# Skip term as a scalar in the frequency product, and a program order for the first six chunks

## The chip, the cores and the metric

The kernel runs on one core of a Trainium2 chip. The core has a matrix engine (PE, with its weight loads PEld), a vector engine (DVE), an activation engine (ACT), a general engine (POOL) and a queue engine (SP). Engines run at the same time, each goes through its own instructions in order, and they meet at semaphores. Transfers are issued from queues (here SP's and POOL's) and done by 16 DMA engines. The metric is the device time of one execution in microseconds (us); the time before is 758.68 us, the median of 3 runs (758.16 to 759.4).

## The reference, cut to what matters

One block of a conditioned network over 2048 positions and 512 channels: a layer norm with a modulation, a state-space convolution with a skip term, a residual, a second layer norm, and a two-layer MLP.

```python
mod = (silu(c) @ w_mod).reshape(1, 6, 1, -1)        # six rows: sa, ca, ga, sb, cb, gb
h = layernorm(x) * (1 + ca) + sa
# the convolution, per channel d:
P = exp(logdA[:, :, None] * l)                       # 128 complex states, 2048 positions
K = einsum("dn,dnl,dn->dl", Cc, P, dB).real          # its kernel
y = irfft(rfft(pad(h)) * rfft(pad(K)))[:L] + h * Dskip
x = x + ga * y
h = layernorm(x) * (1 + cb) + sb
x = x + gb * (mish(h @ w1 + b1) @ w2)                # w1 512x1792, w2 1792x512
```

The skip `h * Dskip` can be had in three ways that are the same in exact arithmetic: added to the output, added to the kernel's first tap (K[0] + Dskip), or added to every frequency of the kernel's transform (a first tap of height Dskip has the constant transform Dskip).

## The kernel before, in words

The kernel is written in Python for a scheduler: each line issues an instruction with tiles, and the scheduler works out the order of each engine from the data it needs and from a priority number (low first), then adds the waits. A tile pool gives each tag a fixed number of buffers; who wants a buffer waits for the last reader of the tile that held it.

**Stages.** (1) Parameters of the state space are prepared on DVE and ACT for each of four blocks b of 128 channels (`params`, stages 0 to 3, `load_s`, `coarse`). (2) The convolution is done in 32 chunks, 8 for each block. (3) The MLP, from about 436 us on, is matmuls with fp32 operands split in two parts.

**A slot.** The loop over k from -1 to 40 is the slot loop. In slot k each step of `ORDER` runs for the chunk k minus its offset:

- `ang` (chunk k+2): PE matmuls that make 2 x 512 angles in PSUM (one buffer of two banks, "pa"), L343 and L347.
- `sin` (k+2): three ACT passes, Abs (L354) and two sines (L138), into the tile `ec` (three buffers).
- `mag` (k+1): two DVE products m2 and m1 (L364, L367).
- `comb` (k): four DVE multiplies of `ec` by the magnitudes (L374 to L378).
- `kgen` (k-1): 64 small PE matmuls that give 16 channels' kernels (L389).
- `ks` (k-1): ACT copies them out of PSUM (L394), and DVE adds the skip to the first tap (L395).
- `ka` (k-1): the first half of the kernel's transform on PE (L406), and `tm` copies it (ACT, L413).
- `gl` (offset 6), `ubu` (7), `ug` (7): load the first half of the input's transform from DRAM (`ud`), do its second half on PE (L522, with a shift term at L529), and scale it on ACT into the tile `ug` (two buffers).
- `ubk` and `prod` (8): the second half of the kernel's transform (PE, tile `pkb`), and the complex product of both on DVE: two multiplies at L556 and a subtraction and an addition.
- `t1`, `invb`, `zl`, `xp`, `inva`: transposes (L563) and the inverse transform, through DRAM, with the residual.

**The input's first half.** Ahead of slot 7 the input x (2048 rows as 16 tiles `XR`) is loaded by 20 transfers (`x_rows`, L189), its mean and variance are taken (`stats`: three quarters by DVE's statistics instructions L671 and L672, the fourth quarter by ACT's accumulating passes L677 and L681), `norm_scales` makes the reciprocal roots by twelve small DVE instructions, `norm` scales each of the 16 tiles (L495), and `ua`, eight groups, does 16 matmuls each (L502), four ACT copies (L506) and eight stores to `ud` from SP (L508). The eight copies of two groups have a buffer each; the third group waits for the first one's stores.

**The modulation.** Each of six rows of 512 needs four loads of w_mod (`mod_load`, L430), four products on PE of two matmuls each (`mod_mm`, L437), a copy (`mod_cp`), four small products (`mod_sum`, L446) and a DVE copy (L447). Rows 3 and 0 are needed for the input's scale, row 5 for the shift (`shift_ratio`, `shift_rows`).

**What sets the order.** `MS` gives each modulation row its slot, `SL` the slots of the parameter stages within a block of eight, `BN`, `NS`, `UO` those of statistics, norms and `ua`. Work dealt out so (`extra`) runs in the groups "misc" and "par". The tables `PRI0` (slots below 7) and `PRI` (from 7 on) shift the priority number of a step within its slot. Every engine's order is then the scheduler's.

Of the kernel before, what the change touches and what calls it, by code (L numbers as in the profile page):

```python
# [10 lines left out]
F32 = mybir.dt.float32  # L11
# [7 lines left out]
P = 128  # L19
# [94 lines left out]
def s4_block(ctx, tc, io, out):  # L114
    nc = tc.nc
    V, A, T = nc.vector, nc.scalar, nc.tensor
# [31 lines left out]
    def view(src, offset, ap):  # L148
        return bass.AP(tensor=src.tensor, offset=src.offset + offset, ap=ap)
# [82 lines left out]
    def params(b, stage):  # L232
# [9 lines left out]
        def split(i, j):  # L242
            hi = PKR[b][:, 2 * i:2 * j:2, :]
            (A.copy if b and SPA else V.tensor_copy)(hi, r[:, 10 + i:10 + j, :])
            V.tensor_sub(PKR[b][:, 2 * i + 1:2 * j:2, :], r[:, 10 + i:10 + j, :], hi)
# [146 lines left out]
    def s_ks(k):  # L392
        KS[k] = gen.tile([P, 256], F32, tag="ks", name=f"ks{k}", bufs=1)
        A.copy(KS[k], PK[k][:, :256])  # L394
        V.tensor_add(KS[k][:, 0:256:64], KS[k][:, 0:256:64], dtap[:, k])  # L395
# [27 lines left out]
    WM, PM = {}, {}  # L423
# [15 lines left out]
    def mod_cp(s):  # L439
        WM[s] = cv.tile([P, D], F32, tag="q2", name=f"mr{s}", bufs=1)  # L440
        A.copy(WM[s], PM[s])

    def mod_sum(s):
        p = bank("pmodp")
        for b in range(NB):
            T.matmul(p[:, b:b + 1], WM[s][:, b * P:b * P + P], mean, start=True, stop=True)  # L446
        V.tensor_scalar(modp[:, s, :], p[:, :NB], float(s in (2, 3)), None, op0=OP.add)  # L447
# [84 lines left out]
    def alt(tag, v):  # L532
        pool = MW["wr"] if "wr" in MW and v % 2 else cv
        return pool.tile([P, 512], F32, tag=tag, name=f"{tag}{v}", bufs=1)

    def s_ug(v):
        b = v // 8
        UG[v] = cv.tile([P, 512], F32, tag="ug", name=f"ug{v}", bufs=NUG).rearrange("p (r c s) -> p r c s", r=4, c=2)
        A.mul(UG[v].rearrange("p r c s -> p c r s"), PU[v].rearrange("p (c r s) -> p c r s", c=2, r=4),
              gd[:, b:b + 1])  # L540
# [7 lines left out]
    def s_prod(v):  # L548
        b = v // 8
        ug = UG[v]  # L550
        q1 = alt("q1", v).rearrange("p (r c s) -> p r c s", r=4, c=2)
        q2 = cv.tile([P, 4, 2, 64], F32, tag="q2", name=f"q2{v}", bufs=1)
        YY[v] = q1
        kv = PKB[v].rearrange("p (c r s) -> p c r s", c=2, r=4)
        for q, c in ((q1, 0), (q2, 1)):
            V.tensor_mul(q, kv[:, c, :, None, :].to_broadcast([P, 4, 2, 64]), ug)  # L556
        V.tensor_sub(q1[:, :, 0], q1[:, :, 0], q2[:, :, 1])
        V.tensor_add(q1[:, :, 1], q1[:, :, 1], q2[:, :, 0])
# [86 lines left out]
    s_sin(0)  # L645
    s_mag(0)
# [44 lines left out]
    at(-1, lambda: nc.sync.dma_start(mf.rearrange("p a b -> p (a b)"), io["mf"]))  # L691
    for g in range(4):
        at(BN[g], stats, g)
    at(NS, norm_scales)
    at(2, lambda: nc.sync.dma_start(mi.rearrange("p a b -> p (a b)"), io["mi"]))
# [90 lines left out]
    for nm, o in ORDER:  # L786
        if nm in ("par", "misc"):
            STEPS.append((nm, nm, 0))
        else:
            STEPS.append((nm, locals()["s_" + nm], o))  # L790

    NAME = {params: "p", load_s: "ls", norm: "nr", ua: "ua", mod_load: "ml", mod_mm: "mm", mod_cp: "mc", mod_sum: "ms",
# [3 lines left out]
    def run(name, k, pos, f, *a):  # L796
        tc.cur_priority = 100000 + int(10000 * (k + (PRI0 if k < KP else PRI).get(name, pos)))
        f(*a)

    def run_extra(k, group, pos):  # L800
        for g, a in extra.get((k, group), []):
            run(NAME.get(g, "ld"), k, pos, g, *a)

    for k in range(-1, last_slot + 1):
        if k == NG + 2:
            mlp_open()
        for i, (nm, f, o) in enumerate(STEPS):
            pos = i / len(STEPS)
            if isinstance(f, str):
                if k >= LATE:  # L810
                    run_extra(k, f, pos)
                continue
            if (0 if k >= 0 else 1) <= k - o < (NG - 4 if f in (s_xp, s_zl, s_inva) else NG):
# [121 lines left out]
_INS = ["A_u", "B_w1", "B_b1", "B_w2", "c", "w_mod"]  # L935
# [34 lines left out]
```

## Time and profile before

| what | value |
|---|---|
| median of 3 runs | 758.68 us (758.16 to 759.4) |
| the profiled execution's own time | 760.26 us |
| its span in the trace | 758.5 us, 14126 instructions |
| busy: PE, DVE, ACT, POOL | 662.4, 434.8, 339.2, 51.7 us |
| weight loads (PEld) | 510.4 us |
| moved by DMA | 82.92 MB |

The span is what the trace covers; what lies around it is 1.8 us. Busy times are sums over the whole span, and the stages have different limits, so they say little by themselves. A line of a timeline has the start in us, the duration of the whole group in us, engine, source line, operation, tiles written and read with their shape, and the count of instructions merged; in brackets stands the idle time ahead of it and what ended that idle time. Matmuls overlap, so a group's duration is less than count by mean. A line of a group has busy us and mean ns of one, then idle time ahead of the group in sum. A line of DMA issues has the count, the size of each and the median us from issue to landing. A line of a stage has its bounds, its length, and for PE, PEld, DVE, ACT and POOL the busy us with the count of instructions, then the granted clock of PE, the DMA engines' share and GB/s.

### The profile page before, as it was taken

The page shows a single profiled execution, that of the slowest core. Times are in us where ns is not written, and L with a number is a line of the kernel's source. Part 1 is how long each engine was busy: PE and PEld are TensorE (multiplying, and loading weights), DVE is VectorE, ACT ScalarE, POOL GpSimd, SP SyncE. Part 2 cuts the span into 40 slices and gives each one's busy share as a digit, 9 for nine tenths or more (in the row PEclk, how much of TensorE's full clock was granted, in tenths as well). Part 3 has the DMA queues.
Part 4 walks back from the last instruction along what each step waited for, and adds up shares of the span by engine and source line. Part 5 has one row for each costly group of instructions (what it writes and reads, how often), then busy time and mean ns, then how long its engine had stood idle before and what let it go on. Part 6 is the DMA issues. An engine that isn't in the chain of part 4 may idle for free.

```text
span 758.5 us, 14126 instructions
## 1 busy us (share of the span) xinstructions
PE 662.4 (87%) x5696; PEld 510.4 (67%) x5696; DVE 434.8 (57%) x900; ACT 339.2 (45%) x529; POOL 51.7 (7%) x111
## 2 busy tenths in 40 slices
PE   0661997899999999999883699999999999999995
PEld 0431435567877878887663278887888888878884
DVE  6598626597999988996562596137211521152113
ACT  3760558555786677665441163232223322232220
POOL 1024002050206020000000000000000000000000
PEclk9875879899999999999997799999999999999998
DMA  9925588653326662654965770003200320002002
GB/s 229 237 97 176 136 186 188 181 135 105 76 63 146 160 178 81 166 153 143 262 174 143 211 254 15 1 4 88 75 1 0 89 79 0 1 11 74 1 1 55
DMA packets 98489, 82.92 MB, mean 109 GB/s; under 512 B 11636, under 2 KB 79992, under 8 KB 97784
## 3 DMA queue, kind: packets, MB, share of 16 engines
q1 hardware_dynamic: 91704, 78.15, 37.6%
q0 software_dynamic: 6720, 3.87, 2.7%
q8 instruction: 45, 0.74, 0.4%
q14 instruction: 20, 0.16, 0.1%
HBM read 54.72 MB, written 25.17 MB: 105 GB/s over the span
## 4 chain that ended last, share of the span: by engine, by line
PE 76%; DMA 7%; DVE 6%; ACT 6%; SPq 3%; issue 2%; POOL 0%; DVEq 0%; ACTq 0%; POOLq 0%
PE pm L864 18%; PE po L882 18%; PE pang L343 4%; PE pub L522 4%; PE pkg L389 4%; PE pka L406 4%; PE pang L347 4%; PE pkb L522 4%; PE pib L571 4%; PE pt L563 2%; PE pmodr L437 2%; ACT ec L354 2%; PE pua L502 1%; DMA raw<-in_par 1%; PE pia L609 1%
## 5 line engine op out<-in xcount | busy, mean ns | idle before, releaser
L871 DVE TENSOR_TENSOR mal<-mh,mah 128x512 fp32r<-128x512 f32 x56 | 38.6, 691 | 178.7 <-ACT mah L870 178.2
L864 PE MATMUL pm<-hh,w1h 128*128 128x512 f32 x448 | 138.6, 390 | 2.2 <-ACT hh L775 1.2
L138 ACT ACTIVATE mh<-pm,b 128x512 f32<-128x512 f32 x56 | 38.5, 690 | 202.5 <-PE pm L864 202.5
L864 PEld LDWEIGHTS pm<-hh,w1h 128*128 128x128 f32 x448 | 83.7, 188 | 21.6 <-ACT hh L775 2.1
L882 PE MATMUL po<-w2h,mah 128*128 128x512 f32 x224 | 87.8, 392 | 0.0
L882 PE MATMUL po<-w2h,mal 128*128 128x512 f32 x224 | 87.7, 391 | 0.0
L882 PE MATMUL po<-w2l,mah 128*128 128x512 f32 x224 | 87.5, 391 | 0.0
L864 PE MATMUL pm<-hh,w1l 128*128 128x512 f32 x224 | 87.2, 389 | 0.0
L406 PE MATMUL pka<-bdk,ks 128*64 128x128 f32 x512 | 39.0, 285 | 17.9 <-DVE ks L395 17.9
L556 DVE TENSOR_TENSOR q<-pkb,ug 128x512 f32<-128x512 f32 x64 | 41.2, 685 | 21.8 <-PE pkb L522 21.6
L374 DVE TENSOR_TENSOR ec<-ec,m 128x1024 f32<-128x1024 f32 x32 | 39.1, 1221 | 20.2 <-ACT ec L138 19.9
L882 PEld LDWEIGHTS po<-w2h,mal 128*128 128x128 f32 x224 | 42.1, 188 | 8.8 <-DVE mal L871 0.3
L864 PEld LDWEIGHTS pm<-hh,w1l 128*128 128x128 f32 x224 | 42.0, 188 | 8.6
L882 PEld LDWEIGHTS po<-w2l,mah 128*128 128x128 f32 x224 | 42.1, 188 | 8.4
L882 PEld LDWEIGHTS po<-w2h,mah 128*128 128x128 f32 x224 | 42.1, 188 | 8.3
L406 PEld LDWEIGHTS pka<-bdk,ks 128*64 128x64 f32 x512 | 29.3, 139 | 24.5 <-DVE ks L395 18.4
L354 ACT ACTIVATE ec<-pang 128x1024 f32<-128x1024 f32 x32 | 33.0, 1030 | 26.6 <-PE pang L343 23.5
L347 PE MATMUL pang<-rnd,oneb 128*128 128x512 bf16 x128 | 43.0, 420 | 0.0
L343 PE MATMUL pang<-ac,s 128*128 128x256 f32 x128 | 31.0, 325 | 13.2 <-ACT ec L138 13.0
L364 DVE TENSOR_TENSOR m<-co 128x1024 f32<-128x1024 f32 x32 | 39.1, 1222 | 2.9 <-ACT co L138 2.4
L571 PE MATMUL pib<-yt,mi 128*128 128x128 f32 x256 | 36.6, 288 | 4.5 <-ACT yt L565 4.5
L343 PE MATMUL pang<-nac,s 128*128 128x256 f32 x128 | 40.2, 397 | 0.0
(165 smaller groups left out, 1140.9 us busy)
## 6 DMA issues: line engine op xcount, KB each, us to landing
ud<-us SPq DMA_DIRECT2D x64, 128.0 KB, 2.4
gu<-ud SPq DMA_DIRECT2D x32, 256.0 KB, 3.5
zd<-z SPq DMA_DIRECT2D x32, 256.0 KB, 2.6
zt<-zd SPq DMA_DIRECT2D x32, 256.0 KB, 4.8
wm<-in_w_mod SPq DMA_DIRECT2D x24, 256.0 KB, 3.5
out<-ot SPq DMA_DIRECT2D x64, 64.0 KB, 1.7
xp<-in_A_u SPq DMA_DIRECT2D x60, 64.0 KB, 2.5
x2d<-xp SPq DMA_DIRECT2D x15, 256.0 KB, 3.7
```

The lines of the kernel that those rows point to most:

```text
L343: T.matmul(p[:, e, 256 * q:256 * q + 256], S12[b, 2 * q + c // 4][:, e, :], w[:, 32 * o:32 * o + 256], start=(w is ac and q == 0), stop=(w ...
L347: T.matmul(p[:, e, :], oneb.to_broadcast([P, P]), rnd[:, z:z + 1].to_broadcast([P, 512]), start=False, stop=False, skip_group_check=True)
L354: A.activation(ang[0], pv, AF.Abs)
L364: V.tensor_mul(m2.rearrange("p d (a b) -> p d a b", a=8), co[:, :, 12:20, None].to_broadcast([P, 16, 8, 8]), co[:, :, None, 20:28].to_broa ...
L374: V.tensor_mul(ec[:, :, :, 32:64], ec[:, :, :, 95:63:-1], m2[:, None, :, 0:32].to_broadcast([P, 2, 16, 32]))
L406: T.matmul(pv[64 * cc:64 * cc + 64, :, o:o + 4], KS[k][:, 64 * m:64 * m + 64], bdk[:, 128 * cc:128 * cc + 128], start=True, stop=True)
L522: T.matmul(pv[:, :, r, :], lh(r), mf[:, 4 * s + r, :].rearrange("p (c s) -> p c s", c=2), start=not started, stop=True, skip_group_check=s ...
L556: V.tensor_mul(q, kv[:, c, :, None, :].to_broadcast([P, 4, 2, 64]), ug)
L571: T.matmul(p[:, P * r:P * r + P], mi[:, 4 * s + r, :], YT[v][:, r, :], start=True, stop=True)
L864: T.matmul(p, w1[wi][:, k, fs], hh[:, hi, k, :], start=(n == 0), stop=(n == 3 * KB - 1))
L871: V.tensor_sub(a[1], h, a[0])
L882: T.matmul(PO[tt][q], a[ai][:, P * q:P * q + P], w2[wi][:, f, :], start=(f == 0 and n == 0), stop=(f == FB - 1 and n == 2))
```

## The change

1. **Skip.** `dtap` with its memset and load, and the add at L395, are gone. A tile `skip` holds Dskip as one value per channel and block. `s_prod` uses it as the scalar of one multiply: (kernel + skip) * input.
2. **Layout of the product.** `ug` keeps PSUM's order of real and imaginary parts, and the product's result is written back into the `ug` tile, which `t1` then reads. Before, it was written into `q1`.
3. **Program order.** The wrapper `InOrder` ties every DVE, ACT and PE instruction to the one issued before it on the same engine, from behind `stats(3)` until slot 6 begins (`KO`). The ties carry no wait; they only fix the engine's order. In these slots the steps follow `FIRST`. From slot 6 on `ORDER` and `PRI` hold; `PRI0` is gone.
4. **Work dealt out by slot.** `stats` of all quarters and `norm_scales` stand ahead of the slots. `NR` deals the norms to slots 0, 0, 1, 1, 2, 3, 3, 3 and `UA` the eight ua groups to slots 1, 1, 2, 3, 3, 4, 5, 5. Modulation rows go to slots 1, 2, 3 (rows 3, 5, 0) and 8, 10, 12 (1, 2, 4), each with its loads one slot before and its copy, sum and DVE copy one, two and three slots behind; before, they were 0, 1, 3 and 6, 8, 9. The shift goes from slot 5 to 6, the loads of the transform's tables `mf` and `mi` from slots -1 and 2 to 3 and 5.
5. **Parameters.** In each block stage 2 goes from slot 0 to 1, stage 3 from 2 to 3, the first `load_s` from 5 to 4.
6. **Loads of x.** Every second transfer of the first load of x is issued from POOL's queue instead of SP's.

```diff
+SL = {"p2": 1, "p3": 3, "ls0": 4, "raw": 2, "p0": 5, "ls1": 8, "co0": 6, "vis": 6}
+MS = [[3, 1], [5, 2], [0, 3], [1, 8], [2, 10], [4, 12]]
+MR = 6
+NR = [0, 0, 1, 1, 2, 3, 3, 3]
+UA = [1, 1, 2, 3, 3, 4, 5, 5]
+KO = 6
+FIRST = [
+    ("kgen", 1), ("ks", 1), ("ang", -2), ("comb", 0), ("mag", -1), ("sin", -2), ("ka", 1), ("tm", 1),
+    ("gl", 6), ("misc", 0), ("par", 0),
+]
...
+            def issue(*a, **kw):
+                ins = f(*a, **kw)
+                if self.key in ordered:
+                    if ordered[self.key] is not None:
+                        tc.add_manual_dep(ins.ins, ordered[self.key].name,
+                                          mybir.DependencyInfo(mybir.DependencyClass.NoSync,
+                                                               mybir.DependencyReason.DATA),
+                                          reason="program order")
+                    ordered[self.key] = ins.ins
+                return ins
...
+    V, A, T = InOrder(nc.vector, "V"), InOrder(nc.scalar, "A"), InOrder(nc.tensor, "T")
...
-    dtap = cst.tile([P, 8 * NB, 4], F32, name="dtap")
-    nc.gpsimd.memset(dtap, 0.0)
-    nc.sync.dma_start(dtap[0:P:32], io["dtap"].rearrange("t (k m) -> t k m", m=4))
+    skip = cst.tile([P, NB], F32, name="skip")
+    nc.sync.dma_start(skip, view(io["A_Dskip"], 0, [[1, P], [P, NB]]))
...
+            q = nc.gpsimd if b is None and a % 2 else nc.sync
...
-        V.tensor_add(KS[k][:, 0:256:64], KS[k][:, 0:256:64], dtap[:, k])
...
+        ug = UG[v].rearrange("p (c x) -> p c x", c=2)
+        y = YY[v] = UG[v].rearrange("p (r c s) -> p r c s", r=4, c=2)
+        V.scalar_tensor_tensor(q1, kv[:, 0:1].to_broadcast([P, 2, 256]), skip[:, b:b + 1], ug,
+                               op0=OP.add, op1=OP.mult)
+        V.tensor_mul(q2, kv[:, 1:2].to_broadcast([P, 2, 256]), ug)
+        V.tensor_sub(y[:, :, 0], rs(q1[:, 0]), rs(q2[:, 1]))
+        V.tensor_add(y[:, :, 1], rs(q1[:, 1]), rs(q2[:, 0]))
...
-    s_sin(0)
-    s_mag(0)
...
+    at(3, lambda: nc.sync.dma_start(mf.rearrange("p a b -> p (a b)"), io["mf"]))
+    stats(3)
+    for key in "VAT":
+        ordered[key] = None
+    s_sin(0)
+    s_mag(0)
+    for g in (1, 2, 0):
+        stats(g)
+    norm_scales()
+    at(5, lambda: nc.sync.dma_start(mi.rearrange("p a b -> p (a b)"), io["mi"]))
...
+        if k == KO:
+            ordered.clear()
```

More of the change, by code (lines that the diff above doesn't have):

```diff
@@ L115, in s4_block, with __init__, __getattr__ @@
     nc = tc.nc
-    V, A, T = nc.vector, nc.scalar, nc.tensor
+    ordered = {}
+    class InOrder:
+        def __init__(self, engine, key):
+            self.engine, self.key = engine, key
+        def __getattr__(self, name):
+            f = getattr(self.engine, name)
+            def issue(*a, **kw):
[8 more added lines that the diff above has]
+                return ins
+            return issue
+    V, A, T = InOrder(nc.vector, "V"), InOrder(nc.scalar, "A"), InOrder(nc.tensor, "T")
     psum = ctx.enter_context(tc.tile_pool(name="psum", bufs=6, space=bass.MemoryType.PSUM))
@@ L243, in split @@
             hi = PKR[b][:, 2 * i:2 * j:2, :]
-            (A.copy if b and SPA else V.tensor_copy)(hi, r[:, 10 + i:10 + j, :])
+            V.tensor_copy(hi, r[:, 10 + i:10 + j, :])
             V.tensor_sub(PKR[b][:, 2 * i + 1:2 * j:2, :], r[:, 10 + i:10 + j, :], hi)
@@ L421, in s4_block @@
     nc.gpsimd.memset(one, 1.0)
-    WM, PM = {}, {}
+    WM, PM, MRW = {}, {}, {}
     mean = cst.tile([P, 1], F32, name="mean")
@@ L439, in mod_cp @@
     def mod_cp(s):
-        WM[s] = cv.tile([P, D], F32, tag="q2", name=f"mr{s}", bufs=1)
-        A.copy(WM[s], PM[s])
+        MRW[s] = cv.tile([P, D], F32, tag="q2", name=f"mr{s}", bufs=1)
+        A.copy(MRW[s], PM[s])
     def mod_sum(s):
@@ L445, in mod_sum, with mod_out @@
         for b in range(NB):
-            T.matmul(p[:, b:b + 1], WM[s][:, b * P:b * P + P], mean, start=True, stop=True)
-        V.tensor_scalar(modp[:, s, :], p[:, :NB], float(s in (2, 3)), None, op0=OP.add)
+            T.matmul(p[:, b:b + 1], MRW[s][:, b * P:b * P + P], mean, start=True, stop=True)
+        PM[s] = p
+    def mod_out(s):
+        V.tensor_scalar(modp[:, s, :], PM[s][:, :NB], float(s in (2, 3)), None, op0=OP.add)
     sab = cst.tile([P, D], BF16, name="sab")
@@ L537, in s_ug @@
         b = v // 8
[L538 to L540 removed]
+        UG[v] = cv.tile([P, 512], F32, tag="ug", name=f"ug{v}", bufs=NUG)
+        A.mul(UG[v], PU[v], gd[:, b:b + 1])
     def s_ubk(v):
@@ L549, in s_prod @@
         b = v // 8
[L550 to L558, printed above, removed]
+        ug = UG[v].rearrange("p (c x) -> p c x", c=2)
+        y = YY[v] = UG[v].rearrange("p (r c s) -> p r c s", r=4, c=2)
+        q1 = alt("q1", v).rearrange("p (c x) -> p c x", c=2)
+        q2 = cv.tile([P, 2, 256], F32, tag="q2", name=f"q2{v}", bufs=1)
+        kv = PKB[v].rearrange("p (c x) -> p c x", c=2)
+        V.scalar_tensor_tensor(q1, kv[:, 0:1].to_broadcast([P, 2, 256]), skip[:, b:b + 1], ug,
+                               op0=OP.add, op1=OP.mult)
+        V.tensor_mul(q2, kv[:, 1:2].to_broadcast([P, 2, 256]), ug)
+        rs = lambda t: t.rearrange("p (r s) -> p r s", r=4)
+        V.tensor_sub(y[:, :, 0], rs(q1[:, 0]), rs(q2[:, 1]))
+        V.tensor_add(y[:, :, 1], rs(q1[:, 1]), rs(q2[:, 0]))
     def s_t1(v):
@@ L690, in s4_block @@
     at(-1, const_loads)
[L691 to L695, printed above, removed]
+    at(3, lambda: nc.sync.dma_start(mf.rearrange("p a b -> p (a b)"), io["mf"]))
[8 more added lines that the diff above has]
+    at(5, lambda: nc.sync.dma_start(mi.rearrange("p a b -> p (a b)"), io["mi"]))
     for i, n in MS:
         for q in range(KB):
-            at(max(n - 1 + q // 2, -1), mod_load, KB * i + q)
-            at(n + q // 2, mod_mm, KB * i + q)
+            at(n - 1, mod_load, KB * i + q)
+            at(n, mod_mm, KB * i + q)
         at(n + 1, mod_cp, i)
-        at(n + 1, mod_sum, i)
+        at(n + 2, mod_sum, i)
+        at(n + 3, mod_out, i)
     at(MR, shift_ratio)
@@ L718, in s4_block @@
         for h in range(2):
-            at(NS, norm, 8 * h + g)
-        at(NS + UO + n // 2, ua, g)
+            at(NR[n], norm, 8 * h + g)
+        at(UA[n], ua, g)
     def mlp_open():
@@ L785, in s4_block @@
     STEPS = []
[L786 to L792, printed above, removed]
+    steps = lambda order: [(nm, nm if nm in ("par", "misc") else globals_[f"s_{nm}"], o) for nm, o in order]
+    globals_ = locals()
+    FS, STEPS = steps(FIRST), steps(ORDER)
+    NAME = {params: "p", load_s: "ls", norm: "nr", ua: "ua", mod_load: "ml", mod_mm: "mm", mod_cp: "mc", mod_sum: "ms", mod_out: "ms",
             shift_ratio: "sr", shift_rows: "sr", stats: "st", norm_scales: "no", coarse_mm: "co", visit: "vi",
@@ L806, in s4_block @@
             mlp_open()
-        for i, (nm, f, o) in enumerate(STEPS):
+        if k == KO:
+            ordered.clear()
+        for i, (nm, f, o) in enumerate(FS if k < KO else STEPS):
             pos = i / len(STEPS)
             if isinstance(f, str):
[L810 to L813, printed above, removed]
+                run_extra(k, f, pos)
+            elif (0 if k >= 0 else 1) <= k - o < (NG - 4 if f in (s_xp, s_zl, s_inva) else NG):
                 run(nm, k, pos, f, k - o)
-        for n in ("par", "misc") if k < LATE else ():
-            run_extra(k, n, 0.99)
         if k == last_slot - 3:
@@ L932, in s4_block @@
         fin_q(3, q, xl)
[L935 removed]
+_INS = ["A_u", "A_Dskip", "B_w1", "B_b1", "B_w2", "c", "w_mod"]
 _PAR = ["A_B_re", "A_B_im", "A_C_re", "A_C_im", "A_A_re", "A_A_im"]
```

18 lines of the change are left out of this document (3 added, 15 removed).

## The prediction

> **What bounds the kernel now.** I read the slices of the span first, then busy time by stage, then the engines' timelines through the first stages, and last SP's queue.
>
> ```profile
> span 758.5 us, 14126 instructions
> PE   0661997899999999999883699999999999999995
> ```
> ```profile
> 49.50:126.14 76.64, 53.85 (x617) 28.18 (x614) 49.59 (x111) 35.77 (x59) 16.22 (x32) 0.80 0.64 163
> 182.83:355.60 172.77, 170.02 (x2602) 140.44 (x2605) 158.92 (x265) 123.85 (x186) 20.49 (x40) 1.00 0.49 128
> ```
>
> The first fence has PE's busy tenths in slices of 19 us: nines from the tenth slice on, but for the passage to the MLP (slices 20 to 23). The second gives for a stretch the busy time of PE, its weight loads, DVE, ACT and POOL, then the granted clock. In the steady stage, from 182.83 on, PE is busy 170.0 of 172.8 us at full clock. There the change can give little, for it adds and removes no matmul. The head is another matter: 76.6 us pass from the first kernel chunk (kgen(0), 49.50) to the sixth (kgen(5), 126.14), with PE busy in 53.9 of them at a mean clock of 0.80.
>
> DVE's timeline says why; the second fence is ACT and PE:
>
> ```profile
> 27.73 0.68 DVE L367 TENSOR_TENSOR m<-co 128x512 f32<-128x512 f32 x1
> 34.60 1.23 DVE L374 TENSOR_TENSOR ec<-ec,m 128x1024 f32<-128x1024 f32 x1 [6.19 <-ACT ec L138]
> 38.08 0.69 DVE L376 SCALAR_TENSOR_TENSOR ec<-ec,m 128x512 f32<-128x512 f32 x1
> 53.85 1.28 DVE L671 BATCH_NORM_STATS2 bst<-xr 128x6 f32<-128x512 f32 x2
> 65.16 7.62 DVE L495 TENSOR_SCALAR xr<-xr,mv,rstd 128x512 f32<-128x512 f32 x16
> ```
> ```profile
> 49.50 1.15 PE L389 MATMUL pkg<-ec 128*32 128x64 f32 x64
> 50.70 0.37 ACT L394 COPY ks<-pkg 128x256 f32<-128x256 f32 x1 [3.12 <-PE pkg L389]
> 72.91 0.69 PE L406 MATMUL pka<-bdk,ks 128*64 128x128 f32 x2 [16.75 <-DVE ks L395]
> 126.14 1.17 PE L389 MATMUL pkg<-ec 128*32 128x64 f32 x64
> 142.91 1.17 PE L389 MATMUL pkg<-ec 128*32 128x64 f32 x64
> 144.33 1.16 PE L522 MATMUL pub<-mf,gu 128*128 128x128 f32 x8
> ```
>
> ACT has the first chunk's ks ready at 51.1. The skip term's small add stands on DVE behind the statistics, the scales and all sixteen norms (53.85 to 72.78), and PE waits 16.75 us for it. Only then can the eight ua groups come, in a heap, and SP must store their rows:
>
> ```profile
> 82.90 24.15 SPq L508 DMA_DIRECT2D ud<-us  x32
> 108.42 23.67 SPq L508 DMA_DIRECT2D ud<-us  x32
> 135.72 1.92 PE L437 MATMUL pmodr<-wm,sc 128*32 128x512 f32 x2 [5.30 <-DMA wm<-in_w_mod]
> 140.49 1.52 PE L437 MATMUL pmodr<-wm,sc 128*32 128x512 f32 x4
> ```
>
> 64 stores at 0.75 us hold SP from 82.9 to 132.1. Weights of the modulation queue behind them (PE waits 5.30 for those), and the first ubu, which needs all of ud, does its products at 144.33.
>
> **The change, part by part.**
>
> *Skip term.* The add at L395 goes, and with it DVE's place between ks and ka. The product takes the scalar instead: one of its two multiplies becomes a three-operand instruction with a pointer.
>
> ```profile
> L556 DVE TENSOR_TENSOR q<-pkb,ug 128x512 f32<-128x512 f32 x64 | 41.2, 685 | 21.8 <-PE pkb L522 21.6
> L467 DVE SCALAR_TENSOR_TENSOR sa_a<-sab,hl,pmod 128x512 f32<-128x512 bf16 x1 | 0.7, 747 | 2.7 <-ACT sab L466 2.7
> ```
>
> The nearest row with a pointer and PSUM costs 747 against 685 ns: 62 ns by 32 chunks is 2.0 us more of DVE at worst, none at best. In the steady stage DVE is busy 158.9 of 172.8 us and PE has 2.7 us idle, so neither reaches the end: nothing.
>
> *UG keeps the product.* A UG buffer is now free only when the transposes t1 have read it. In a steady slot:
>
> ```profile
> 182.83 1.17 PE L389 MATMUL pkg<-ec 128*32 128x64 f32 x64
> 185.44 0.69 ACT L539 ACTIVATE ug<-pub,gd 128x512 f32<-128x512 f32 x1 [1.02 <-DVE ks L395]
> 187.08 0.60 PE L563 MATMUL pt<-ident,q 128*128 128x128 f32 x4
> 187.28 1.02 ACT L354 ACTIVATE ec<-pang 128x1024 f32<-128x1024 f32 x1 [1.15 <-PE pang L343]
> 190.62 1.17 PE L389 MATMUL pkg<-ec 128*32 128x64 f32 x64
> ```
>
> ug(v+2), at 185.44, moves behind t1(v), which ends at 187.68. Its reader is the product a slot of 7.8 us (182.83 to 190.62) later; that slack hides it: nothing. Without the cover, with ug still queued ahead of Abs, ACT is 187.68 + 0.69 - 187.28 = 1.1 us late in each slot: rival C.
>
> *The start in program order.* DVE now does mag(0), twelve statistics and the scales, and only then comb(0): 28.4 (27.73 + 0.68) and 11.3 (53.85 to 65.16) make 39.7, against 34.60 before. comb(0) takes 4.2 (34.60 to 38.77), so kgen(0) can come at 43.9. ACT's statistics of the fourth quarter may stand ahead of the first sines as well, and PE does ang(2) before kgen(0): I take 46, between 44 and the 49.5 of before. x has to be there in time for this: two statistics take 1.4 with what is between them, so the last four start at 28.4 + 4 x 1.4 = 34.
>
> *Slots 1 to 5.* Each has one kernel chunk; the ua groups are 2, 1, 2, 1, 2; three modulation rows, the norms and params lie between. DVE's work, cut up, fits into each slot. What is left is a chain over PE and ACT:
>
> ```profile
> 129.33 1.09 PE L406 MATMUL pka<-bdk,ks 128*64 128x128 f32 x14
> 52.04 1.03 ACT L354 ACTIVATE ec<-pang 128x1024 f32<-128x1024 f32 x1
> 115.49 2.27 PE L502 MATMUL pua<-xr,bdu 32*64 32x512 f32 x24
> 117.49 3.52 ACT L506 COPY us<-pua 128x512 f32<-128x512 f32 x7 [1.08 <-PE pua L502]
> ```
>
> kgen and ang on PE 3.2 (126.14 to ka at 129.33), the three sine passes 3.0 (1.03 each, overlapping a little), the copies tm and mod_cp 0.5 each, eight ua copies 4.0 (seven took 3.52), ks 0.4: 11.6. With one ua group it is 9.6. Three and two of them: 54, so kgen(5) stands at 100. Low end: PE's own work alone. Five times kgen, ang, ka (4.3), three modulation rows of eight matmuls (0.38 each at 140.49; 9) and eight ua of 16 matmuls (1.5 each; 12) are 42.5: kgen(5) at 88.5. High end: the pace at which chunks came while ua copies crowded ACT:
>
> ```profile
> 100.17 0.17 DVE L395 TENSOR_TENSOR ks<-ks,dtap 128x4 f32<-128x4 f32 x1 [5.55 <-ACT ks L394]
> 114.00 0.17 DVE L395 TENSOR_TENSOR ks<-ks,dtap 128x4 f32<-128x4 f32 x1 [6.45 <-ACT ks L394]
> ```
>
> 13.8 by five is 69: kgen(5) at 115. I take 100, for that chain follows the order as it is written out.
>
> *To the first ubu.* kgen(6) follows a slot with table loads and eight exponentials; the like slot later takes 10.6 (206.20 to 216.80), and ubu's products start 1.4 behind kgen (142.91 to 144.33): 112. The other condition is the rows of ud. Slot 5's first ua copy is 4.4 ahead of kgen(5), at 96; sixteen stores of 0.75, landing 2.4 and gu 3.5 give 114. I take 115.
>
> ```profile
> 206.20 1.17 PE L389 MATMUL pkg<-ec 128*32 128x64 f32 x64
> 216.80 1.17 PE L389 MATMUL pkg<-ec 128*32 128x64 f32 x64
> ud<-us SPq DMA_DIRECT2D x64, 128.0 KB, 2.4
> gu<-ud SPq DMA_DIRECT2D x32, 256.0 KB, 3.5
> mf<-in_mf SPq DMA_DIRECT2D x1, 2048.0 KB, 11.6
> mi<-in_mi SPq DMA_DIRECT2D x1, 2048.0 KB, 8.1
> ac<-in_ac POOLq DMA_DIRECT2D x1, 512.0 KB, 7.7
> s<-pk POOLq DMA_DIRECT2D x16, 16.0 KB, 2.8
> ```
>
> *Moved rows and loads.* Modulation rows 1, 2 and 4 go to slots 8, 10 and 12. Of row 1, six matmuls stood ahead of 144.33 (135.72 and 140.49) and now come behind it: 3.4 at the clock of those rows, half of it at the full clock; I take 1.5. mf and mi move from the start to slots 3 and 5, among the stores: nothing while the stores keep ahead of the copies, 20 us of transfers if not (rival B). skip's load is 512 single floats in front of the second raw load, where dtap had four long rows: 0 to 2, I take 1. Params move by a slot in each block: DVE has 13.9 us free in 172.8, nothing.
>
> *The sum.* 144.3 - 115 = 29.3, less 1.5 and 1: 26.8 us. The profiled execution took 760.26 (its span 758.5), so 733.5 for such a one; it stands 1.6 above the median of the runs, 758.68, which gives **732**. With kgen(5) at 88.5 the stores allow ubu(0) at 102: 40 us gained, 719. With 115 it is at 127: 15 gained, 744.
>
> **The rivals.**
>
> *B: the stores stay the bound.* The first ua copy stands 7.6 behind kgen(0), at 54. From there 64 stores of 0.75 (48), mf 11.6, mi 8.1 and 5.9 to gu make 128 for the first ubu; with eight weight loads at two stores' time each (12) 140. Middle 134: 10.3 less 2.5 gained, **751**. For it: SP needed 49 us for the stores alone, and its queue is in order: the third raw load, in slot 2, must wait there for params of slot 3. Against: spread over slots of 54 us the stores have gaps to hide in.
>
> *C: the longer life of UG.* 1.1 us in each of 22 slots (172.8 / 7.8) is 24; half of that covered, 12: **744**. Against: ACT has 49 of 172.8 us free, and ACT's order behind the sixth chunk is dealt out anew with this wait known.
>
> *D, the other side: x comes late.* Half of x's twenty loads go to POOL's queue, and DVE in program order cannot pass the statistics. Every microsecond that x lands after 34 is one for all that follows; from 34 + 26.8 = 61 on the kernel is slower. If the ten landed one after the other, at the 7.7 us of a POOL load in this window, from 3 on, they end at 80, 46 late: **778**. Against: POOL's loads overlap, and between 52 and 72 us, with DVE full of statistics and norms, sixteen small ones landed in 2.8 us each (the last row above).
>
> The Trainium skill speaks for D: by "SBUF — State Buffer", section "SBUF: two separate sides", GpSimd cannot write the descriptors of its own DMAs while DVE runs a fast two-port operation, and the remedy named is the queue that these loads leave. The row of 2.8 us does not show such a hold-up.
>
> *E: nothing gained.* If program order adds 5 us to each of the five slots, because ACT, waiting for a us buffer, keeps ks and the sines behind it, kgen(5) is where it was: **759**.
>
> **How the numbers follow.** Forecast 0.60, B 0.20, C 0.09, D 0.06, E 0.05. The forecast's own range is 719 to 744. To hold 8 in 10 I keep 719 below and go over B to 754 above; D, E and tails are left out. A difference under 0.2% (1.5 us) counts as no change. Faster is the forecast, B and C less their tails, 0.87; same is most of E, 0.04; slower is D and the rest of E, 0.09.
>
> **What would show it.** No PE wait near 17 us ahead of the first ka; kgen(5) between 88 and 115 and the first ubu between 102 and 127; no stretch of DVE with all statistics and norms in one piece; the first store ahead of 65; a steady slot of 7.8 us. Wrong: DVE idle on x's loads ahead of the statistics; ACT waiting on ud for over 15 us in sum; PE waiting on gu or weights past 127; steady slots over 8.2.

## The result, and the profile after

The changed kernel takes 737.96 us (median of four runs, 736.02 to 740.05) against 758.42 of the kernel before (757.17 to 759.4): a ratio of 0.973, with a 95% interval of 0.969 to 0.977. The sum said 732, and faster. The sign is right, the time lies in the range, and the gain is 20.5 us where the sum had 26.8. The profiled execution of after took 740.05, its span is 738.2.

The first fence holds the head of the page and PE's busy tenths; the second, busy time by stage (columns as in the prediction).

```profile
span 738.2 us, 14029 instructions
PE   0449877999999999999955899999999999999995
```
```profile
54.66:111.38 56.72, 48.63 (x632) 27.41 (x637) 55.93 (x108) 36.39 (x60) 16.28 (x32) 0.89 0.75 182
161.17:334.00 172.83, 167.91 (x2567) 139.39 (x2586) 157.08 (x242) 121.57 (x185) 21.43 (x42) 1.00 0.51 132
```

The steady stage is what it was. From kgen(0) to kgen(5) pass 56.7 us instead of 76.6, and in them DVE is busy 55.9. But that stretch begins 5.2 us later than before, at 54.66 instead of 49.50. All three engines' instructions now bear the line of the wrapper, L126, so one reads by tile names. DVE's and PE's timelines, and ACT's last cast of the shift rows:

```profile
19.46 0.42 DVE L126 TENSOR_TENSOR raw<-raw 128x256 f32<-128x256 f32 x1 [7.49 <-DMA raw<-in_par]
36.77 1.83 DVE L126 TENSOR_TENSOR m<-co 128x1024 f32<-128x1024 f32 x2 [2.84 <-ACT co L126]
50.92 1.94 DVE L126 TENSOR_TENSOR ec<-ec,m 128x1024 f32<-128x1024 f32 x2
```
```profile
111.38 1.47 PE L126 MATMUL pkg<-ec 128*32 128x64 f32 x64
118.78 1.17 PE L126 MATMUL pkg<-ec 128*32 128x64 f32 x64
122.31 0.80 PE L126 MATMUL pang<-ac,s 128*128 128x256 f32 x2 [2.35 <-ACT ec L126]
128.04 0.50 PE L126 MATMUL pang<-ac,s 128*128 128x256 f32 x2 [2.03 <-ACT ec L126]
131.40 1.69 PE L126 MATMUL pub<-mf,gu 128*128 128x128 f32 x8
134.05 1.17 PE L126 MATMUL pkg<-ec 128*32 128x64 f32 x64
337.33 1.17 PE L126 MATMUL pkg<-ec 128*32 128x64 f32 x64
```
```profile
129.43 0.61 ACT L126 CAST sab<-sa_a 128x512 bf16<-128x512 f32 x1
```

In the first fence the second raw tile is late (19.46; before, the first multiply on it stood at 11.50), and with it all that follows up to the first comb (50.92). In the second, the first ubu comes only at 131.40, 12.6 behind kgen(6). The last chunk, kgen(31), stands at 337.33; before, it stood here:

```profile
355.53 1.17 PE L389 MATMUL pkg<-ec 128*32 128x64 f32 x64
```

So 18.2 us are gained ahead of kgen(31), and the rest of the span differs by 2.1 (402.97 before, 400.87 after). That rest has the last products in it, whose form the change alters; from the last product on, where the code is the same, it is 350.2 and 350.3. Over the fourteen kernels profiled here the rest behind kgen(31) lies between 397.7 and 403.0. Each kernel's runs spread by 2 to 10 us. So below I read the time by its interval, and use the starts in the trace to see which step moved.

SP's queue, the stores of ua's rows and the first loads of gu:

```profile
64.47 12.07 SPq L531 DMA_DIRECT2D ud<-us  x16
79.42 4.62 SPq L531 DMA_DIRECT2D ud<-us  x7
85.99 19.61 SPq L531 DMA_DIRECT2D ud<-us  x25
108.94 11.72 SPq L531 DMA_DIRECT2D ud<-us  x16
123.63 0.94 SPq L537 DMA_DIRECT2D gu<-ud  x2
```

The stores are four bursts with gaps now, and end at 120.7 instead of 132.1.

### The profile page after: what moved, and what is told of

Read it like the earlier page. It is cut to its first block, busy times and chain, and to the rows that moved or that the text cites. A ratio compares the mean times of both kernels' runs of the same rounds, so it can differ in the third digit from the quotient of the medians.

```text
span 738.2 us, 14029 instructions
## 1 busy us (share of the span) xinstructions
PE 651.5 (88%) x5667; PEld 509.2 (69%) x5696; DVE 433.3 (59%) x868; ACT 336.1 (46%) x529; POOL 56.5 (8%) x120
## 4 chain that ended last, share of the span: by engine, by line
PE 73%; DVE 12%; DMA 7%; ACT 3%; issue 2%; SPq 1%; DVEq 0%; ACTq 0%
PE pm L126 21%; PE po L126 20%; PE pang L126 6%; PE pub L126 5%; PE pkg L126 4%; PE pkb L126 4%; PE pib L126 3%; DVE ec L126 3%; PE pka L126 3%; DVE raw L126 3%; DMA raw<-in_par 2%; PE pt L126 2%; PE pia L126 1%; PE pln L126 1%; DMA wm<-in_w_mod 1%
## 5 line engine op out<-in xcount | busy, mean ns | idle before, releaser
L126 DVE TENSOR_TENSOR mal<-mh,mah 128x512 fp32r<-128x512 f32 x56 | 38.6, 691 | 181.2 <-ACT mah L126 180.8
L126 PE MATMUL pm<-hh,w1h 128*128 128x512 f32 x448 | 139.5, 393 | 1.1 <-ACT hh L126 1.1
L126 ACT ACTIVATE mh<-pm,b 128x512 f32<-128x512 f32 x56 | 38.5, 690 | 202.5 <-PE pm L126 201.7
L126 DVE TENSOR_TENSOR ec<-ec,m 128x1024 f32<-128x1024 f32 (+1 forms) x96 | 97.2, 1040 | 13.9 <-ACT ec L126 13.6
L126 PEld LDWEIGHTS pm<-hh,w1h 128*128 128x128 f32 x448 | 84.7, 190 | 19.7 <-ACT hh L126 1.5
L126 ACT ACTIVATE ec<-pang 128x1024 f32<-128x1024 f32 x64 | 65.0, 1033 | 58.6 <-PE pang L126 58.6
L126 PE MATMUL po<-w2h,mah 128*128 128x512 f32 x224 | 87.8, 392 | 0.0
L126 PE MATMUL pm<-hh,w1l 128*128 128x512 f32 x224 | 87.7, 391 | 0.0
L126 PE MATMUL po<-w2h,mal 128*128 128x512 f32 x224 | 87.6, 391 | 0.0
L126 PE MATMUL po<-w2l,mah 128*128 128x512 f32 x224 | 87.5, 391 | 0.0
L126 DVE TENSOR_TENSOR m<-co 128x512 f32<-128x512 f32 (+1 forms) x64 | 59.7, 951 | 4.0 <-ACT co L126 3.6
L126 PEld LDWEIGHTS pm<-hh,w1l 128*128 128x128 f32 x224 | 42.4, 189 | 8.7
L126 PEld LDWEIGHTS po<-w2h,mal 128*128 128x128 f32 x224 | 42.1, 188 | 8.7 <-DVE mal L126 0.3
L126 PEld LDWEIGHTS po<-w2l,mah 128*128 128x128 f32 x224 | 42.1, 188 | 8.4
L126 PEld LDWEIGHTS po<-w2h,mah 128*128 128x128 f32 x224 | 42.1, 188 | 8.3
L126 PE MATMUL pkg<-ec 128*32 128x64 f32 x2048 | 38.5, 226 | 4.9 <-DVE ec L126 4.2
L126 PEld LDWEIGHTS pkg<-ec 128*32 128x32 f32 x2048 | 33.3, 111 | 13.3 <-DVE ec L126 3.9
L126 PE MATMUL pang<-nac,s 128*128 128x256 f32 x128 | 41.3, 405 | 0.0
L126 PE MATMUL pang<-ac,s 128*128 128x256 f32 x128 | 31.1, 325 | 10.9 <-ACT ec L126 9.8
L126 PE MATMUL pkb<-mf,gk 128*128 128x128 f32 x256 | 37.1, 289 | 3.2 <-ACT gk L126 3.2
L126 PE MATMUL pka<-bdk,ks 128*64 128x128 f32 x512 | 35.3, 280 | 4.2 <-ACT ks L126 4.2
L126 DVE SCALAR_TENSOR_TENSOR q<-pkb,skip,ug 128x512 f32<-128x512 f32 x32 | 23.9, 746 | 24.6 <-PE pkb L126 24.6
```

The source lines that it names most:

```text
L126: ins = f(*a, **kw)
```

## The experiments

Times in us; the ratio is to runs of the kernel before on the same chip (medians 757.47, 757.93 and 758.12 in the three groups); the last four columns are the starts in one profiled execution (that of after, 740.05, is the longest of its four runs). They vary on the same code: with nothing changed ahead of it, kgen(0) stands at 54.66 in after and at 53.46 in shift_early, and the step from kgen(0) to kgen(5) takes 55.0 to 57.4 in the eight kernels that have the same work in it. Differences of 2 us in these columns show nothing by themselves.

| kernel | median | ratio, 95% | kgen(0) | kgen(5) | first ubu | kgen(31) |
|---|---|---|---|---|---|---|
| before | 758.42 | | 49.50 | 126.14 | 144.33 | 355.53 |
| after | 737.96 | 0.969 to 0.977 | 54.66 | 111.38 | 131.40 | 337.33 |
| x_on_sp | 736.47 | 0.970 to 0.975 | 54.77 | 110.77 | 130.77 | 336.30 |
| skip_late | 734.45 | 0.967 to 0.973 | 54.40 | 109.46 | 129.45 | 334.86 |
| both_loads | 736.80 | 0.970 to 0.976 | 54.15 | 109.19 | 129.93 | 334.99 |
| shift_early | 734.57 | 0.968 to 0.973 | 53.46 | 108.73 | 123.97 | 329.26 |
| skip_alone | 750.76 | 0.987 to 0.994 | 49.87 | 116.90 | 136.13 | 347.97 |
| old_skip | 736.58 | 0.968 to 0.974 | 53.65 | 110.79 | 132.78 | 337.01 |
| no_order | 750.21 | 0.987 to 0.994 | 53.65 | 122.82 | 140.42 | 347.55 |
| stats_on_dve | 731.49 | 0.963 to 0.969 | 48.10 | 103.18 | 124.09 | 329.81 |
| norms_on_act | 742.64 | 0.976 to 0.983 | 53.33 | 112.09 | 131.91 | 337.68 |
| stats_on_dve_pool_x | 735.72 | 0.966 to 0.975 | 56.74 | 111.74 | 131.72 | 337.11 |
| stats_and_shift | 728.93 | 0.959 to 0.966 | 48.51 | 105.86 | 122.65 | 328.20 |
| stats_shift_norms | 732.06 | 0.961 to 0.969 | 48.52 | 106.87 | 124.87 | 330.41 |

### Which load makes the second raw tile late

Two suspects: POOL's queue, which now carries half of x, and skip's load of 512 single floats. Three kernels undo the one, the other, and both.

x_on_sp:

```diff
-            q = nc.gpsimd if b is None and a % 2 else nc.sync
+            q = nc.sync
```


> All loads of x go on SP's queue again; nothing else of the changed kernel differs. Theory Q (POOL's loads of x share the DMA engines with SP's queue, and the second raw load arrives late for it): the first multiply on the second raw tile starts at 11.5 to 13 us instead of 19.5, psel on PE 7 to 8 us earlier, and the time falls by 6 to 8 us, to 730 to 732. Theory K (the skip load of 512 single floats, which stands ahead of the second raw load on SP's queue, makes it late): the multiply stays at 18 to 20 us and the time at 737 to 739. A third way: the multiply is early, but the statistics on DVE then wait for x, and less than 3 us are left of the gain.

skip_late: skip's load stands behind all of x.

```diff
-    nc.sync.dma_start(skip, view(io["A_Dskip"], 0, [[1, P], [P, NB]]))
...
+    nc.sync.dma_start(skip, view(io["A_Dskip"], 0, [[1, P], [P, NB]]))
     nc.sync.dma_start(bdk, io["bdk"])
```


> The load of skip is issued behind all loads of x; POOL's queue still takes half of x. Theory K: the first multiply on the second raw tile starts at 11.5 to 13 us, the time falls to 730 to 732. Theory Q: the multiply stays between 17 and 19.5 us, the time within 2 us of 738.

both_loads: both edits.

> All loads of x on SP's queue and the load of skip behind them. By Q as by K the first multiply on the second raw tile starts at about 11.5 us and the time is 730 to 732; if Q alone is right this one and the one with x on SP's queue agree within 1.5 us, if K alone is right this one and the one with skip late agree within 1.5 us.

The first multiply on the second raw tile, in x_on_sp, skip_late and both_loads:

```profile
13.13 0.42 DVE L126 TENSOR_TENSOR raw<-raw 128x256 f32<-128x256 f32 x1 [3.10 <-DMA raw<-in_par]
```
```profile
19.21 0.42 DVE L126 TENSOR_TENSOR raw<-raw 128x256 f32<-128x256 f32 x1 [6.96 <-DMA raw<-in_par]
```
```profile
11.96 0.43 DVE L126 TENSOR_TENSOR raw<-raw 128x256 f32<-128x256 f32 x1 [1.34 <-DMA raw<-in_par]
```

Taking x off POOL's queue brings the tile 6.3 earlier (19.46 to 13.13) or 7.3 (19.21 to 11.96); moving skip's load, 0.3 or 1.2. In the other kernels with x on both queues this multiply stands between 17.9 and 20.7, so the 0.3 and 1.2 are not told apart from nothing. Theory Q holds for the tile, and skip's load costs no more than it was priced at. The DMA issues of the first 30 us (number, size, median us to landing), of after and then of x_on_sp, show the same:

```profile
xr<-in_A_u POOLq DMA_DIRECT2D x6, 256.0 KB, 10.1
xr<-in_A_u SPq DMA_DIRECT2D x6, 256.0 KB, 18.8
raw<-in_par SPq DMA_DIRECT2D x2, 384.0 KB, 9.9
```
```profile
xr<-in_A_u SPq DMA_DIRECT2D x12, 256.0 KB, 8.7
raw<-in_par SPq DMA_DIRECT2D x2, 384.0 KB, 6.6
```

With two queues, what stays on SP takes 18.8 instead of 8.7: the two share one set of DMA engines, and bulk that has time on one queue delays a load that has none on the other. The Trainium skill has the mechanism, in "DMA: Bandwidth & Descriptors", section "Queues, rings and completion order": each DMA engine takes turns between the queues that have work for it, a packet at a time. The rows (18.8 for 8.7, 9.9 for 6.6) agree with the taking of turns; that the turns go by packet, no run here shows.

But the 730 to 732 that Q promised did not come, nor any time that can be told apart: the three intervals overlap that of after, and kgen(0) has not moved (54.15 to 54.77). Skip_late's 734.45 lies between the times of Q and K, and the third way, DVE waiting for x, was not it either. DVE's timeline of both_loads says why:

```profile
27.93 1.83 DVE L126 TENSOR_TENSOR m<-co 128x1024 f32<-128x1024 f32 x2 [7.44 <-ACT co L126]
35.21 0.17 DVE L126 TENSOR_SCALAR nmr<-sq 128x4 f32<-128x4 f32 x1 [5.45 <-ACT junk L126]
40.26 0.17 DVE L126 TENSOR_SCALAR mv<-sq 128x4 f32<-128x4 f32 x1 [2.58 <-ACT junk L126]
50.41 1.95 DVE L126 TENSOR_TENSOR ec<-ec,m 128x1024 f32<-128x1024 f32 x2
```

The products m come 8.8 earlier, at 27.93, and then DVE waits 8.0 for sums that ACT takes of the fourth quarter of x. In the changed kernel ACT did that work while everything waited for the raw tile.

### All statistics on DVE

stats_on_dve is both_loads and this:

```diff
-SA = 1
+SA = 0
-    stats(3)
     for key in "VAT":
         ordered[key] = None
...
-    for g in (1, 2, 0):
+    for g in (3, 1, 2, 0):
         stats(g)
```


> As the kernel with all loads of x on SP's queue and skip late, but with all sixteen statistics on DVE, none on ACT. Theory W (with the early second raw load, DVE in its order waits 8 us for ACT's sums of the fourth quarter, 5.45 and 2.58, which eats what the early load gained): these waits go, four statistics (3.4 us) come, kgen(0) at 49 to 51 instead of 54.2, and if the start is passed on to the end the time is 731 to 734. Theory X (DVE then waits for x itself): kgen(0) stays at 53 to 56, with DVE idle on loads of x, and the time at 736 to 738.

DVE's m and first comb, and PE's kgen(0):

```profile
26.93 1.83 DVE L126 TENSOR_TENSOR m<-co 128x1024 f32<-128x1024 f32 x2 [7.44 <-ACT co L126]
44.36 1.94 DVE L126 TENSOR_TENSOR ec<-ec,m 128x1024 f32<-128x1024 f32 x2
```
```profile
48.10 1.96 PE L126 MATMUL pkg<-ec 128*32 128x64 f32 x64 [7.10 <-DVE ec L126]
```

W holds: the waits are gone, kgen(0) stands at 48.1 (W had 49 to 51), and the time is 731.5. Against both_loads, from which only the statistics differ, kgen(31) is 5.2 earlier, the median 5.3 lower, and the intervals do not overlap. stats_on_dve_pool_x makes the same edit but leaves the loads alone:

> The changed kernel with all sixteen statistics on DVE, its loads left as they are (half of x on POOL's queue, skip ahead of the second raw load). Theory R (the late second raw load costs nothing in the changed kernel only because ACT does its statistics in that idle time): DVE's products m come at 35 to 37 as in the changed kernel, four statistics more stand behind them, kgen(0) at 56.5 to 59 instead of 54.7 and of the 48.1 that the same kernel has with all loads of x on SP, time 739 to 742. Theory T (all that mattered was ACT's share of the statistics): kgen(0) at 48 to 51, time 731 to 734.

kgen(0) is at 56.74, as R has it: with the raw tile late, four more statistics only add. So the load and ACT's sums cover each other, and only taking both away brings something. R's time fell: two us of a later start were gone by kgen(5) (111.74 against 111.38), and the median is 735.7. That is within what this step varies by on the same code (55.0 to 57.4).

### The skip term, the ties and the dealing, one at a time

skip_alone is the kernel before with the skip term of the change and nothing else (`s_ug`, `s_prod` and the load too are as in the change):

```diff
         A.copy(KS[k], PK[k][:, :256])
-        V.tensor_add(KS[k][:, 0:256:64], KS[k][:, 0:256:64], dtap[:, k])
...
-        for q, c in ((q1, 0), (q2, 1)):
-            V.tensor_mul(q, kv[:, c, :, None, :].to_broadcast([P, 4, 2, 64]), ug)
+        V.scalar_tensor_tensor(q1, kv[:, 0:1].to_broadcast([P, 2, 256]), skip[:, b:b + 1], ug,
+                               op0=OP.add, op1=OP.mult)
+        V.tensor_mul(q2, kv[:, 1:2].to_broadcast([P, 2, 256]), ug)
```

> The kernel before with the skip scalar and the longer life of UG alone; order, loads and dealing as before. Theory O (the order holds the first chunks: the second comb stands behind the sixteen norms on DVE, whether or not the small add does): PE's wait of 16.75 us ahead of the first ka goes, yet kgen(1) stays at 82 to 85, and the time at 755 to 759. Theory A (the add was the cause of the late start): kgen(1) comes at 68 to 72 and the time falls to 740 to 746.

Neither theory held: 750.76, a gain of 7.2. DVE's norms, then PE, and last the end of comb(1) on DVE in the kernel before:

```profile
65.51 7.39 DVE L493 TENSOR_SCALAR xr<-xr,mv,rstd 128x512 f32<-128x512 f32 x16
```
```profile
66.12 2.05 PE L500 MATMUL pua<-xr,bdu 32*64 32x512 f32 x8 [4.56 <-DVE xr L493]
74.96 1.17 PE L388 MATMUL pkg<-ec 128*32 128x64 f32 x64
```
```profile
43.95 0.68 DVE L376 SCALAR_TENSOR_TENSOR ec<-ec,m 128x512 f32<-128x512 f32 x1
```

O's premise was wrong: with three buffers for `ec`, the combs of chunks 0, 1 and 2 stand ahead of the statistics, comb(1) has ended at 44.6 (in skip_alone at 44.8), and the one behind the norms is comb(3). What held kgen(1) was PE's own order. There it stands behind the first ka and two ua groups. PE's queue, no longer shut by ka, starts on the ua groups at 66.1 instead of 79.1, while the norms run, and so kgen(1) comes 9.2 earlier. It is not where theory A has it (68 to 72), because the ua groups ahead of it wait for norms (4.56, then 2.05).

old_skip is the changed kernel with the same edit undone: the add to ks is back, the product has two plain multiplies, and UG is free after it.

```diff
         A.copy(KS[k], PK[k][:, :256])
+        V.tensor_add(KS[k][:, 0:256:64], KS[k][:, 0:256:64], dtap[:, k])
```

> The changed kernel with the skip term of before: the add to ks on DVE, its four-row load, the product by two plain multiplies, UG free after the product. Program order and dealing as in the changed kernel. Theory L (in program order the add keeps DVE until ACT's copy of ks, so each slot of the start is 2 us longer, and 2 us of DVE work is not where it counts later): kgen(5) at 119 to 123 instead of 111.4, time 744 to 750. Theory N (the skip term costs nothing in either form): 736.5 to 739.5. If rival C of the prediction (the longer life of UG) cost anything, the stretch from 161 us to the end would be shorter here than in the changed kernel by more than 2 us.

N holds: 736.58, kgen(31) at 337.01 against 337.33. PE's longest wait for the add is now

```profile
71.11 1.97 PE L126 MATMUL pka<-bdk,ks 128*64 128x128 f32 x16 [3.49 <-DVE ks L126]
```

3.5, not 16.75. For rival C: from 161 to the end this kernel is 3.7 shorter (573.3 against 577.0), more than the 2 that I had set as the mark. From kgen(10) to kgen(31) it is 175.7 against 176.2. Of the other 3.2, 2.5 lie between kgen(31) and the last product (48.1 against 50.5), where the last UG tiles are still in use. But that stretch does not go with the form of the product: before, with the old one, has 52.8 there, and the twelve kernels with the new one 49 to 52. So the 12 us of C did not come; a cost of 1 or 2 is neither shown nor excluded.

no_order is the changed kernel without the ties:

```diff
-    for key in "VAT":
-        ordered[key] = None
```


> The changed kernel without the ties in program order; the list and the slots of the first six chunks are kept as due times for the planner. Theory P (the ties bring the gain): DVE does most norms in a piece again, kgen(1) comes after 75, time 746 to 756. Theory D (the new dealing over slots brings it): kgen(5) between 105 and 114, time within 3 us of 738.

P holds on the time: 750.21; kgen(1) came a little earlier than it said, at 72.86. Ten norms go in a piece again on DVE, and 48 of the stores follow in one run on SP's queue:

```profile
65.72 4.65 DVE L126 TENSOR_SCALAR xr<-xr,mv,rstd 128x512 f32<-128x512 f32 x10
```
```profile
85.97 48.38 SPq L531 DMA_DIRECT2D ud<-us  x48
```

They end at 134.3 and the first ubu is at 140.42: rival B's picture. The ties spread the ua groups, and with them the stores. Together: without ties, the skip edit and the new dealing give 7.7; the skip edit alone gives 7.2; with ties, 20.5 with the skip edit and 21.4 without it. So on top of the new dealing the ties add 12.8, and with them the skip edit brings no time that can be told apart. Ties without the new dealing were not run.

### The first ubu: the shift rows

shift_early changes one entry of `PRI`, the due time of `shift_ratio` and `shift_rows`:

```diff
-"sr": 1.575
+"sr": 0.45
```


> One number of the changed kernel differs: the planner's due time of the shift rows is 1.125 slots earlier, ahead of the first ubu instead of behind it. Theory S (the first ubu waits at 131 us for the third cast of sab, at 130.04): the casts end by 126, the first ubu's products start at 125 to 128, and the time falls by 2 to 5 us, to 733 to 736. Theory G (ubu stands behind ang, and ang behind ACT's exponentials and sines): the first ubu stays at 130 to 132 and the time within 1.5 us of 738.

ACT's last cast of sab, and PE's ubu:

```profile
121.52 0.61 ACT L126 CAST sab<-sa_a 128x512 bf16<-128x512 f32 x1
```
```profile
123.97 1.16 PE L126 MATMUL pub<-mf,gu 128*128 128x128 f32 x8 [0.16 <-DMA gu<-ud]
```

S holds: the casts end at 122.1 instead of 130.0, ubu comes 7.4 earlier (a little earlier than S had it), kgen(31) 8.1. But 3.0 of this stood already at kgen(6) (115.82 against 118.78), ahead of the shift rows; theirs are the 4.5 by which the step from kgen(6) to ubu is shorter (8.15 against 12.62). Now gu is the last to come (0.16), and with it the stores. The median gain is 3.4 (734.57), and the intervals of the two ratios overlap; how much of the 4.5 reaches the end, these runs don't settle.

### Norms on ACT, and what is best

norms_on_act moves eight of the sixteen norms to ACT:

```diff
     def norm(j):
+        if j >= 8:
+            A.activation(XR[j], XR[j], AF.Identity, scale=rstd[:, j:j + 1], bias=nb[:, j:j + 1])
+            return
```


> The changed kernel with eight of the sixteen norms on ACT (scale and bias by pointer) and one small instruction more on DVE. Theory V (DVE, busy 55.9 of the 56.7 us from kgen(0) to kgen(5), sets that stretch): it loses eight norms of 0.47 us, 3.7, and the stretch falls to 52.5 to 54, the time to 734 to 736. Theory H (the chain over PE and ACT that the prediction summed sets it): ACT gains eight instructions of about 0.6 us, the stretch grows to 58 to 62, and the time is 738 to 742.

The stretch from kgen(0) to kgen(5) by busy time, then a wait of PE and one of ACT in it:

```profile
53.33:112.09 58.76, 50.52 (x636) 29.45 (x636) 53.79 (x104) 41.59 (x68) 16.31 (x32) 0.85 0.73 175
```
```profile
89.41 1.96 PE L126 MATMUL pkg<-ec 128*32 128x64 f32 x64 [3.40 <-DVE modp L126]
```
```profile
102.36 0.58 ACT L126 COPY us<-pua 128x512 f32<-128x512 f32 x1 [2.80 <-DMA ud<-us]
```

V fell. DVE has 2.1 less to do and ACT 5.2 more, and the stretch is 2.0 longer, with the time at 742.64. By itself this does not say whether DVE was the bound, for the work went to ACT. The changed kernel's own trace says it, in the end of comb(5) on DVE, ACT's wait for a store of ua's rows, and PE's ka behind it:

```profile
96.84 1.22 DVE L126 TENSOR_TENSOR ec<-ec,m 128x1024 f32<-128x1024 f32 x1
```
```profile
102.61 0.59 ACT L126 COPY us<-pua 128x512 f32<-128x512 f32 x1 [3.82 <-DMA ud<-us]
```
```profile
103.52 1.09 PE L126 MATMUL pka<-bdk,ks 128*64 128x128 f32 x16 [3.18 <-ACT ks L126]
```

Comb(5) has ended at 98.1, 13.3 ahead of kgen(5), which needs it. Within the stretch PE waited for a comb once, 0.47 us ahead of kgen(2). So DVE was busy because it worked ahead, and what held PE's ka in that slot was ACT, held by the stores. H has the stretch right (58 to 62); its time, 738 to 742, is just missed, and the trace shows waits across three engines and the stores rather than one chain.

stats_and_shift joins stats_on_dve and shift_early; stats_shift_norms adds the norms on ACT.

> All loads of x on SP's queue, skip late, all statistics on DVE, and the shift rows due ahead of the first ubu. If the two gains add (kgen(0) 6 us earlier, and the first ubu one third cast earlier): first ubu at 117 to 120, time 726 to 729. If the one hides the other: first ubu at 122 to 125 and the time 731 to 734.

> The same with eight norms on ACT. If DVE still sets the slots: 3 us less than without, first ubu at 114 to 117, time 723 to 726. If another wait (ACT on the stores, PE on weights, SP's queue) takes its place: within 1.5 us of the one without.

The first is the fastest kernel here: 728.93, a ratio of 0.962 (0.959 to 0.966), below after's interval and not told apart from stats_on_dve (0.963 to 0.969). The time is where the gains add (726 to 729), the first ubu (122.65) where one hides the other (122 to 125). Step by step both gains are there: kgen(0) at 48.51, and 9.2 from kgen(6) to ubu where stats_on_dve has 12.9. What was lost lies between, in the 57.4 from kgen(0) to kgen(5), which neither edit touches and which stats_on_dve does in 55.1. So whether they add, one execution each does not settle. The norms on ACT give nothing here either: 732.06, where 723 to 726 had been possible.

## Why the prediction was right, and where it was wrong

Faster, for the reason given: the small add, the norms in one piece and the stores in one heap did make the head long, and a program order took them apart. Of the signs named, these came: no wait near 17 us ahead of a ka (in the stretch from 54 to 112, 4.2 in two, longest 3.2); kgen(5) at 111.4, between 88 and 115; first store at 64.5, ahead of 65; norms and statistics apart; a steady slot of 7.8. One did not: the first ubu, at 131.4 instead of 102 to 127. The terms of the sum, in the profiled execution:

| step | predicted | measured |
|---|---|---|
| kgen(0) | 46 | 54.66 |
| kgen(0) to kgen(5) | 54 | 56.72 |
| kgen(5) to kgen(6) | 10.6 | 7.40 |
| kgen(6) to the first ubu | 4.4 | 12.62 |
| first ubu, in sum | 115 | 131.40 |
| first ubu to the end | 616.7 | 606.8 |

The first four errors are 8.7, 2.7, -3.2 and 8.2, together 16.4 too early. The last gives 9.9 back: 2.5 that I charged and that did not come, 4.1 because kgen(7) now stands 2.65 behind the first ubu instead of 6.7, 1.2 up to kgen(31), and 2.1 behind it. What is left is 6.5: 740.05 instead of 733.5. Nothing of these 9.9 was worked out ahead, so that much of the nearness to 732 is luck: the four errors alone would have made 749.9, close to rival B's 751 without B's cause.

*Skip term: right.* The product of three operands took 746 ns a piece where 747 was borrowed:

```profile
L126 DVE SCALAR_TENSOR_TENSOR q<-pkb,skip,ug 128x512 f32<-128x512 f32 x32 | 23.9, 746 | 24.6 <-PE pkb L126 24.6
```

old_skip shows no cost. What the step did not say is that the wait it removes has two cures, either of them enough for that wait: in skip_alone ka no longer waits for DVE, in old_skip 3.5 at most. Only the ties also took the stores apart.

*UG keeps the product: right as far as the runs tell*, nothing from kgen(10) to kgen(31).

*The start in program order: wrong, and the main miss.* "28.4 and 11.3 make 39.7" took the place of m from before; m came at 36.77 and ended at 38.60, 10.2 late. The second raw tile was 8.0 late (19.46 for 11.50); about 1 of the rest is ACT's statistics, which stand between psel and m (m is at 35.56 in stats_on_dve_pool_x, without them). I had priced "skip's load of 512 single floats in front of the second raw load" at 0 to 2 and found no other reason: the load's own cost was 1.2 at most, and the 6.3 to 7.3 came from x on POOL's queue, which I had weighed for x alone (rival D), not for what else was in flight. And the allowance for ACT's statistics ahead of the first sines, 2 us, hid a second condition of 8.0 that appears as soon as the first is gone. With both gone, comb(0) starts at 44.36 with sixteen statistics; 39.7 and four statistics more (3.4, measured) are 43.1, 1.3 less. So the sum of that step was sound to about 1 us, and its two inputs were not.

*Slots 1 to 5: right in size* (56.7 for 54), and in the main in mechanism: "DVE's work, cut up, fits into each slot" has DVE busy for 55.9 of 56.7, but working ahead (comb(5) ends 13.3 ahead of kgen(5)). The chain over PE and ACT left out one link that only rival E had, ACT's wait for the stores (3.8).

*To the first ubu: a condition was missing.* The two that I named were met: kgen(6) at 118.8, and the stores done 9.3 behind kgen(5) with gu issued at 123.6, which at its 3.2 to landing is 15.4 behind kgen(5) where I had 14. The third, the shift rows, ended at 130.0, and PE's angle matmuls, which stand ahead of ubu in its order, at 130.9; before, the shift rows were done at 128.5, well ahead of 144.33, and so I did not look. With them early (shift_early), 4.5 of the 8.2 go. The change moved them by a slot, and "Moved rows" named only the other rows.

*Rivals.* B: its premise was half wrong, for mf and mi were issued at 32.1 and 32.6, free of the ties, not among the stores; without the ties it is what happens. C: its 12 us did not come. D: DVE waited for no x at all, and POOL's loads landed in 10.1, sooner than SP's 18.8. The rule of the Trainium skill quoted there ("SBUF — State Buffer", section "SBUF: two separate sides") did not show in these rows; they hardly try it, for while POOL issued these loads (3.2 to 14.9) DVE was busy for 5.0 of 11.7 us. E: ACT waited for a us buffer once, 3.8 us, and kept ks and a ka behind it (3.2), not 5 in each slot.

## What to carry to other kernels

When loads move to a second queue, price first what else is in flight: the loads with no slack on the old queue pay, not the moved ones. When an early step is late, list every condition of the next one and its time, for a wait that is taken away uncovers the next in line, here twice. A busy engine that works ahead is not the bound: ask when its result is needed. Two edits aimed at one wait don't add: cost each with the other in place.

## What was not expected of the hardware

The DMA traffic of the first 30 us ran at 225 GB/s with x on two queues, and at 224 before, with x on one. So the second queue brought no rate, only another order: loads of raw landed in a median of 9.9 instead of 5.7. And the stretch behind the last product, the same code each time, took from 348.6 to 351.7 us in fourteen profiled executions. Its mean granted clock does not explain that: 348.6 went with 0.96 and 350.8 with 0.97.
